# Two memory columns fewer, one guess fewer, and memory V turned by a transposing DMA, in a fused S5 scan and memory transformer kernel

## The chip, the cores and the metric

The kernel runs on one core of a Trainium2 chip. The metric is the device time of one execution in microseconds (us). A time is the median of an execution's repeats with the lowest and highest beside it. The span of a profile is some 1.7 us shorter than the time of the same execution.

Engine names: PE is TensorE (matmuls), PEld its weight loads, DVE VectorE, ACT ScalarE, POOL GpSimd, SP SyncE, which issues most DMAs here. "SPq" in a profile line is SP's sequencer.

## The reference, cut to what matters

```python
# A: S5 scan.  x is 2048 x 1024
h_t = Lam_bar * h_{t-1} + B_bar x_t ;  y = 2 Re(h C^T) + x * Dskip
# B: memory transformer.  64 segments of 32 rows, 8 memory rows, 32 heads x 128
mem = mem0
for s in range(64):
    h = concat([mem, x[32*s : 32*s+32]])            # 40 rows
    q, k, v = h @ Wq, h @ Wk, h @ Wv                # per head
    o = softmax(mask(q k^T / sqrt(128))) v  @ Wo
    mem = o[:8]; outs.append(o[8:])
return concat([y, concat(outs)], axis=-1)
```

Part B looks sequential. The kernel guesses each segment's memory with a linear formula from the segment means, computes all segments at once, checks the guess at the end, and only if the check fails branches into a slow general path. With these inputs the branch is never taken into that path.

## The kernel before

The memories are columns of a tile `memT` beside the 2048 columns of x. There are `NM` = 73 of them: 66 that belong to groups (22 groups of three segments) and 7 that are shared. Only 71 memories really exist; two columns are fillers. Three places multiply by these columns. The q and k projections have a tail of 201 = 128 + 73 columns. The memory V products have 73, and the guess products 64.

```python
NTL = 3 * NG; NMX = 7; NM = NTL + NMX               # 66, 7, 73
...
    def v_mem(self, hb, w=None):                     # memory V of a block of four heads
        k = self.k
        w = w or self.load_wv(hb)
        p = k.ps("P")
        for h in range(4):
            for c in range(KC):
                k.PE.matmul(p[:, h * NM:(h + 1) * NM], w[:, c, h * 128:(h + 1) * 128], self.memT[:, c, :], ...)
        vm = self.vmp.tile([128, 4, NM], BF16, name="b_vm", bufs=1)
        k.copy("v", vm[:], p[:, 0:4 * NM].rearrange("p (h n) -> p h n", h=4))
        yield
        pt = k.ps("P", (128, 1024), BF16)
        for h in range(4):                           # columns become rows: four PE transposes
            k.PE.transpose(pt[0:NM, h * 128:(h + 1) * 128], vm[:, h, :], k.ident[:])
        st = self.next_st()
        k.copy("v", st[0:NM, 0, :, 0:E], pt[0:NM, 0:512].rearrange("p (h e) -> p h e", h=4))
        sv = st[:, 0, :, :].rearrange("p h e -> p (h e)")
        k.SP.dma_start(self.vx[hb][64:64 + NMX, :], sv[0:NMX, :])
        k.SP.dma_start(self.vt[hb][:], sv[NMX:NM, :])
        yield
```

Attention then loads V of a head pair (two heads) from DRAM. For the first two head pairs the load begins with a zero fill of the 29 padding rows, by another DMA:

```python
    def load_v(self, hp):
            ...
            if hp < 2:                               # GW = 99: rows 99..127, 29 of them
                z = self.vx[0][T + 32:T + 32 + 128 - GW, 0:2 * EW].unsqueeze(1).to_broadcast([128 - GW, NG, 2 * EW])
                k.tc.keep_in_program_order(k.SP.dma_start(vt[GW:128, :, :], z))
            ...
            k.tc.keep_in_program_order(k.SP.dma_start(vt[0:GX, :, :], self.vx[hb]...))   # b_v <- b_vx
            k.SP.dma_start(vt[GX:GW, :, :], self.vt[hb]...)                              # b_v <- b_vt
```

The memory V of blocks 0 and 1 is computed before attention starts, that of blocks 2 to 7 inside it.

The scheduler moves independent instructions within an engine's stream, so the order on the chip is not the order of the source everywhere.

Of the kernel before, what the change touches and what calls it, by code (L numbers as in the profile page):

```python
# [33 lines left out]
NTL = 3 * NG  # L34
NMX = 7
NM = NTL + NMX
# [300 lines left out]
class PartB:  # L337
    def __init__(self, k, x, mem0, Wq, Wk, Wv, Wo, out):
        self.k = k
        self.x, self.mem0, self.out = x, mem0, out  # L340
        self.Wf = [w.rearrange("(c p) h e -> p c (h e)", p=128) for w in (Wq, Wk, Wv)]
        self.Wo = Wo.rearrange("h e d -> e h d")
        self.vx = [k.drp.tile([NSLOT, 4 * EW], BF16, name=f"b_vx{i}") for i in range(HB)]
        self.vt = [k.drp.tile([NTL, 4 * EW], BF16, name=f"b_vt{i}") for i in range(HB)]
        self.on = [k.drp.tile([T, 1024], BF16, name=f"b_on{i}") for i in range(4)]
        self.tn = [k.drp.tile([NR, 1024], BF16, name=f"b_tn{i}") for i in range(4)]
        c = k.cst
        self.m0T = c.tile([128, KC, M], BF16, name="b_m0T")
        self.gx = c.tile([128, KC, NM], BF16, name="b_gx")
        self.vmp = c  # L350
        self.xbar = c.tile([128, KC, NSEG], BF16, name="b_xbar")
        self.ogT = c.tile([128, H, NSEG], BF16, name="b_ogT")
        self.accE = c.tile([128, HP * NU], FP32, name="b_accE")
        self.accR = c.tile([128, HP * 2 * NG], FP32, name="b_accR")
        self.flag = c.tile([1, 1], I32, name="b_flag")
# [19 lines left out]
    def fill(self, tmp):  # L375
        k = self.k
        z = tmp.tile([32, 4 * EW], BF16, name="b_xr", bufs=4)
        k.V.memset(z[:], 0.0)
        for hb in range(HB):
            k.SP.dma_start(self.vx[hb][64 + NMX:GX, :], z[0:GX - 64 - NMX, :])  # L380
            k.SP.dma_start(self.vx[hb][T + 32:NSLOT, :], z[0:32, :])
        for q in range(4):
            k.SP.dma_start(self.tn[q][NM:NR, 0:4 * EW], z[0:NR - NM, :])
            k.SP.dma_start(self.tn[q][NM:NR, 1024 - 4 * EW:1024], z[0:NR - NM, :])
# [116 lines left out]
    def og(self, hb, w, tag="R"):  # L501
        k = self.k
        p = k.ps(tag)
        late = tag != "R"
        for h in range(4):
            for c in range(KC):
                mm = k.PE.matmul(p[:, h * NSEG:(h + 1) * NSEG], w[:, c, h * 128:(h + 1) * 128], self.xbar[:, c, :], start=(c == 0), stop=(c == KC - 1))
                if late and h == 0 and c == 0:
                    k.tc.keep_in_program_order(mm)
        k.copy("s" if late else "v", self.ogT[:, hb * 4:(hb + 1) * 4, :], p[:, 0:4 * NSEG].rearrange("p (h s) -> p h s", h=4))  # L510
# [7 lines left out]
    def guess(self, pool):  # L518
        k = self.k; V, PE = k.V, k.PE
        pg = k.ps("S")  # L520
        for q in range(4):
            wo = self.wog.pop(0)
            for dc in range(2):
                c = 2 * q + dc
                for h in range(H):
                    PE.matmul(pg[:, c * NSEG:(c + 1) * NSEG], wo[:, h, dc * 128:(dc + 1) * 128], self.ogT[:, h, :], start=(h == 0), stop=(h == H - 1))
# [4 lines left out]
        V.tensor_copy(m[:, :, NMX + 3:NM], pv[:, :, 1:NSEG])  # L531
# [3 lines left out]
        V.tensor_copy(gx[:, :, 2:NTL - 1], pv[:, :, 1:NSEG])  # L535
        V.tensor_copy(gx[:, :, NTL - 1:NM], pv[:, :, 0:1].to_broadcast([128, KC, NMX + 1]))
        yield


    def v_mem(self, hb, w=None):  # L540
# [6 lines left out]
        vm = self.vmp.tile([128, 4, NM], BF16, name="b_vm", bufs=1)  # L547
        k.copy("v", vm[:], p[:, 0:4 * NM].rearrange("p (h n) -> p h n", h=4))
        yield
        pt = k.ps("P", (128, 1024), BF16)  # L550
        for h in range(4):
            k.PE.transpose(pt[0:NM, h * 128:(h + 1) * 128], vm[:, h, :], k.ident[:])
# [4 lines left out]
        k.SP.dma_start(self.vt[hb][:], sv[NMX:NM, :])  # L557
# [7 lines left out]
    def qk_zero(self, i):  # L565
        V = self.k.V
        for t in self.qk[i]:
            V.memset(t[:, :, 64 + NMX:GX], 0.0)
            V.memset(t[:, :, 21 * GP + 64:21 * GP + GX], 0.0)
            V.memset(t[:, :, 0:NG * GP].rearrange("p h (g n) -> p h g n", n=GP)[:, :, :, GW:GP], 0.0)  # L570
            V.memset(t[:, :, NG * GP:QW], 0.0)
# [9 lines left out]
    def proj(self):  # L581

        k = self.k; PE = k.PE
        for hp in range(HP):
# [5 lines left out]
            for i in range(2):  # L590
                t = self.qk[hp % 2][i]
                p = k.ps("P")
                for hh in range(2):
                    for c in range(KC):
# [3 lines left out]
                k.copy("v", t[:, :, 0:64], pv[:, :, 0:64])  # L598
                k.copy("v", t[:, :, 21 * GP:21 * GP + 64], pv[:, :, 64:128])
                k.copy("v", t[:, :, 64:64 + NMX], pv[:, :, 128:128 + NMX])  # L600
                k.copy("v", t[:, :, 0:NG * GP].rearrange("p h (g n) -> p h g n", n=GP)[:, :, :, GX:GW],
                       pv[:, :, 128 + NMX:NS].rearrange("p h (g j) -> p h g j", j=3))
# [45 lines left out]
    def att_back(self, blocks):  # L648
# [24 lines left out]
        if b0 + n == 2 * NG:  # L673
# [8 lines left out]
            k.SP.dma_start(tn[NTL:NM, cs], ov[64:64 + NMX, 0, :])  # L682
# [112 lines left out]
    def check(self):  # L795
# [9 lines left out]
        sq = pool.tile([128, 2, KC, NM], FP32, name="c_sq", bufs=1)  # L805
        df = pool.tile([128, 4, NM], FP32, name="c_df", bufs=1)
        for half in range(2):
            cs = slice(4 * half, 4 * half + 4)
            p = k.ps("P")
            for c in range(4):  # L810
                for h in range(H):
                    PE.matmul(p[:, c * NM:(c + 1) * NM], self.wo[half][:, h, c * 128:(c + 1) * 128], self.omT[:, h, 0:NM],
                              start=(h == 0), stop=(h == H - 1))
            pv = p[:, 0:4 * NM].rearrange("p (c n) -> p c n", c=4)
# [4 lines left out]
        ss = pool.tile([128, 2, NM], FP32, name="c_ss", bufs=1)  # L819
# [5 lines left out]
        for i in range(2):  # L825
            PE.matmul(pd[0:NM, i:i + 1], ss[:, i, :], onef[:], start=True, stop=True)
        t2 = small("c_t2", 2)
        V.memset(t2[:], 0.0)
        V.tensor_copy(t2[0:NM, :], pd[0:NM, 0:2])
# [145 lines left out]
def kernel_main(tc, A_x, A_Lre, A_Lim, A_Bre, A_Bim, A_Cre, A_Cim, A_logdt, A_Dskip, B_x, B_mem0, B_Wq, B_Wk, B_Wv, B_Wo, out,  # L975
                force=False, dbg=None):
    with ExitStack() as ctx:
# [128 lines left out]
        for n, (hp, u) in enumerate(at):  # L1106
            if n == 12:
                k.SP.dma_start(wo0[:], b.Wo[:, :, 0:512])
            if hp % 2 == 0 and 2 < hp + 2 < HP:
                if u == 4:  # L1110
                    vm = b.v_mem(hp // 2 + 1)
                if u in (4, 6):
# [109 lines left out]
```

## Time and profile before

| | before |
|---|---|
| time, median of 3 (lowest to highest) | 1247.11 us (1246.69 to 1247.39) |
| span of the profile | 1245.3 us |
| PE busy | 1234.2 us (99%) |
| DVE, ACT, POOL busy | 54%, 21%, 22% |
| stage 1 of the scan starts on PE | 35.7 us |
| attention | about 440 to 1060 us |
| last matmul ends | 1239.28 us |

From the page of the kernel before: the busy line of its first part, then the two lines of the chain of work that ended last (by engine, then by line).

```profile
PE 1234.2 (99%) x8270; PEld 662.5 (53%) x8342; DVE 667.7 (54%) x1250; ACT 263.4 (21%) x631; POOL 275.8 (22%) x407
...
PE 99%; issue 0%; DVE 0%
PE psP L64 82%; PE psU L64 9%; PE psS L64 3%; PE psO L64 2%; PE psR L64 2%; DVE b_xe L91 0%; DVE b_ost L91 0%; DVE a_n L962 0%; DVE hpb L105 0%; DVE ones L102 0%
```

Both say the same: the kernel is a queue of matmuls. Only less PE work, or less idle time of PE, makes it shorter. The view of waits on PE has one entry of any size, early in the kernel (columns: us in total, times, longest).

```profile
PE psR L64 <- DVE hpb L105: 1.3, 1, 1.3
```

The timeline of PE around one block's transposes (columns: start, us, engine, line, operation, output<-input, shapes, count) gives what a transpose costs in the stream. A duration includes the pipeline's depth, so the cost is read from one start to the next: four transposes take 571.10 - 570.88 = 0.22 us, 55 ns each, not 219 ns.

```profile
570.71 0.33 PE L64 MATMUL psO<-b_v,b_m 128*128 128x129 bf16 x3
570.88 0.39 PE L64 MATMUL psP<-ident,b_vm 128*73 128x128 bf16 x4
571.10 0.60 PE L64 MATMUL psP<-b_xe,b_wk 128*128 128x201 bf16 x5
```

SP's timeline in the same place shows the slack for the DMAs that follow. The memory V of a block is stored at 571.92 and 572.27 us, SP issues nothing between 573.4 and 589.0 us, and V is loaded only at 592.31 us.

```profile
571.92 0.30 SPq L64 DMA_DIRECT2D b_vx<-b_vst  x1
572.27 0.32 SPq L64 DMA_DIRECT2D b_vt<-b_vst  x1
...
572.98 0.40 SPq L64 DMA_DIRECT2D b_wv<-in_B_Wv_dram  x1
589.03 2.01 SPq L64 DMA_DIRECT2D b_on<-b_ob  x2
...
592.31 0.45 SPq L64 DMA_DIRECT2D b_v<-b_vx  x1
```

Two more stretches turned out to matter, and the prediction did not look at them. The first is SP's timeline at the start of attention: the first V load and its zero fill (together `b_v<-b_vx x2`) hold SP for 16.42 us, directly after the stores of memory V.

```profile
465.02 0.27 SPq L64 DMA_DIRECT2D b_vx<-b_vst  x1
465.34 0.29 SPq L64 DMA_DIRECT2D b_vt<-b_vst  x1
465.73 0.26 SPq L64 DMA_DIRECT2D b_v<-b_vt  x1
466.03 16.42 SPq L64 DMA_DIRECT2D b_v<-b_vx  x2
```

```profile
SPq L1156 <- SPq L1156: 2.8, 1, 2.8
```

### The profile page before, as it was taken

The numbers are of one execution on the slowest core, as the hardware profiler recorded it, in microseconds if no ns is written. First come the engines' busy times: TensorE is split into PE (matmuls) and PEld (weight loads), VectorE is DVE, ScalarE is ACT, GpSimd is POOL, SyncE is SP. The second block draws the span as 40 slices with busy tenths as digits, with TensorE's granted clock in tenths as the row PEclk, the third lists the DMA queues.
The fourth block names the chain that finished last, engine by engine and source line by source line (L and its number), as shares of the span: only waits on it lengthen the run. The fifth ranks groups of instructions, "written<-read, shape, count | busy, mean of one in ns | idle before, by whom it ended". The sixth has DMA issues, their size and how long they took to land.

```text
span 1245.3 us, 20124 instructions
## 1 busy us (share of the span) xinstructions
PE 1234.2 (99%) x8270; PEld 662.5 (53%) x8342; DVE 667.7 (54%) x1250; ACT 263.4 (21%) x631; POOL 275.8 (22%) x407
## 2 busy tenths in 40 slices
PE   9999999999999999999999999999999999999998
PEld 5444444444455555556666656555665554446444
DVE  4688899998711124666666666666666641001000
ACT  5344444443310000211112111111211110000000
POOL 4111331212332321322222222222222220000000
PEclk9999999999999999999999999999999999999999
DMA  9965444554898734664454545545553379407000
GB/s 248 272 191 147 131 135 127 144 155 107 242 322 248 249 116 95 196 170 124 96 145 108 144 108 120 132 92 121 120 142 92 65 211 230 107 18 153 17 26 19
DMA packets 316246, 176.83 MB, mean 142 GB/s; under 512 B 138874, under 2 KB 301550, under 8 KB 316150
## 3 DMA queue, kind: packets, MB, share of 16 engines
q1 hardware_dynamic: 294054, 147.95, 47.8%
q10 hardware_dynamic: 21072, 24.38, 5.9%
q0 software_dynamic: 1024, 3.17, 0.7%
q8 instruction: 66, 1.08, 0.4%
q14 instruction: 30, 0.25, 0.1%
HBM read 89.14 MB, written 53.17 MB: 114 GB/s over the span
## 4 chain that ended last, share of the span: by engine, by line
PE 99%; issue 0%; DVE 0%
PE psP L64 82%; PE psU L64 9%; PE psS L64 3%; PE psO L64 2%; PE psR L64 2%; DVE b_xe L91 0%; DVE b_ost L91 0%; DVE a_n L962 0%; DVE hpb L105 0%; DVE ones L102 0%
## 5 line engine op out<-in xcount | busy, mean ns | idle before, releaser
L64 PE MATMUL psP<-b_xe,b_wq 128*128 128x480 bf16 (+1 forms) x1280 | 247.7, 343 | 0.1
L64 PE MATMUL psP<-b_xe,b_wk 128*128 128x480 bf16 (+1 forms) x1280 | 247.7, 343 | 0.0
L64 PE MATMUL psP<-b_wv,b_xe 128*128 128x512 bf16 (+2 forms) x1033 | 223.4, 372 | 0.8
L644 POOL TENSOR_TENSOR b_m<-b_e,maskB 99x396 bf16<-99x396 bf16 x160 | 139.8, 874 | 338.5 <-ACT b_e L641 338.5
L641 ACT ACTIVATE b_e<-psS 99x396 bf16<-99x396 f32 x176 | 88.2, 501 | 536.7 <-PE psS L64 533.4
L64 PEld LDWEIGHTS <-b_wk 128*128 128x128 bf16 x1280 | 119.4, 98 | 94.2
L64 PEld LDWEIGHTS <-b_wq 128*128 128x128 bf16 x1280 | 118.7, 98 | 87.7
L64 PEld LDWEIGHTS <-b_xe 128*128 128x128 bf16 x1056 | 101.8, 98 | 119.1 <-DVE b_xe L91 0.2
L91 DVE CAST b_k<-psP 128x480 bf16<-128x480 f32 (+1 forms) x192 | 97.4, 528 | 100.9 <-PE psP L64 100.9
L91 DVE CAST b_q<-psP 128x480 bf16<-128x480 f32 (+1 forms) x192 | 97.4, 528 | 93.1 <-PE psP L64 91.5
L64 PEld LDWEIGHTS <-b_ol 128*128 128x128 bf16 x864 | 84.3, 98 | 94.4
L64 PE MATMUL psU<-a_xT,a_bt 128*128 128x512 bf16 x493 | 113.9, 379 | 1.1
L64 PE MATMUL psP<-t,a_hl 128*128 128x512 bf16 x496 | 112.1, 379 | 0.8
L91 DVE CAST b_ost<-psP 128x512 bf16<-128x512 f32 (+1 forms) x17 | 11.5, 676 | 177.4 <-PE psP L64 176.3
L64 PE MATMUL psP<-wo,b_ol 128*128 128x512 bf16 (+1 forms) x440 | 91.9, 364 | 0.4
L64 PE MATMUL psP<-t,b_ol 128*128 128x512 bf16 x408 | 91.7, 379 | 0.4
L280 POOL TENSOR_SCALAR a_tt<-a_pr,a_tabf 128x1 f32<-128x1 f32 x48 | 34.1, 710 | 243.2 <-DVE a_pr L275 243.2
L661 DVE TENSOR_TENSOR b_ob<-psO,b_accR 99x384 bf16<-99x384 f32 x160 | 85.9, 553 | 2.4 <-DVE b_accR L660 0.4
L89 ACT ACTIVATE b_vst<-psP 128x512 bf16<-128x512 f32 x126 | 71.9, 589 | 71.3 <-PE psP L64 59.9
L267 DVE TENSOR_TENSOR a_pr<-psU,a_tabf 128x2048 f32<-128x2048 f32 x32 | 73.0, 2282 | 15.7 <-PE psU L64 14.0
L64 PEld LDWEIGHTS <-a_bt 128*128 128x128 bf16 x512 | 49.2, 98 | 57.6
L64 PEld LDWEIGHTS <-a_hl 128*128 128x128 bf16 x512 | 49.0, 98 | 56.7
(200 smaller groups left out, 962.7 us busy)
## 6 DMA issues: line engine op xcount, KB each, us to landing
b_v<-b_vx SPq DMA_DIRECT2D x16, 1122.0 KB
b_wv<-in_B_Wv_dram SPq DMA_DIRECT2D x16, 1024.0 KB
b_vx<-b_vst ACTq DMA_DIRECT2D x24, 544.0 KB
b_on<-b_ob SPq DMA_DIRECT2D x15, 720.0 KB
a_hs<-a_h SPq DMA_DIRECT2D x32, 256.0 KB
b_wog<-in_B_Wo_dram SPq DMA_DIRECT2D x4, 2048.0 KB
b_wq<-in_B_Wq_dram SPq DMA_DIRECT2D x16, 512.0 KB
b_wk<-in_B_Wk_dram SPq DMA_DIRECT2D x16, 512.0 KB
```

The source lines that it names most:

```text
L64: r = f(*a, **kw)
L89: self.S.activation(out, in_, ACT.Copy)
L91: self.V.tensor_copy(out, in_)
L267: V.tensor_tensor(pr[:], u[:].unsqueeze(1).to_broadcast([128, 2, 2, TB]), view(t3, [[TB + 1, 2], [TB + 1, 2], [1, TB]]), ALU.mult)
L280: G.tensor_scalar(tt[:, j:j + 1], w[:, j, TB - 1:TB], t3[:, 1, TB:TB + 1], None, ALU.mult)
L641: k.S.activation(e[:], s[0:GW, :, :, 0:GW], ACT.Exp, scale=float(E) ** -0.5, accum_out=self.accE[0:GW, i:i + 1])
L644: k.G.tensor_tensor(m[0:GW, 0:4 * GP].rearrange("p (a b q) -> p a b q", a=2, b=2)[:, :, :, 0:GW], e[:], mask[0:GW, :, :].unsqueeze(2).to_b ...
L661: V.tensor_tensor(self.ob[:, b0:b0 + n, :], o[0:GW, 0:n, 0:E], r.unsqueeze(2).to_broadcast([GW, n, E]), ALU.mult)
```

## The change

The intent is to take work from PE. (1) The two filler columns go: 71 memory columns instead of 73. (2) The last segment's guess isn't needed: 63 guess columns instead of 64. (3) For six of the eight head blocks the four PE transposes are replaced by a store of V to DRAM, a transposing DMA back, and the stores. Because the filler columns are gone, memory V is no longer one contiguous run of rows, so its store becomes three (`store_t`).

```diff
-NM = NTL + NMX
+NT4 = NMX + 4
+NM = NMX + NSEG                     # 71
+NO = NTL + NMX                      # 73, for the check
 ...
+        self.vmt = [k.drp.tile([E, 512], BF16, name=f"b_vmt{i}") for i in range(HB)]
 ... fill(): eight small stores of ones for the filler rows of vt
-    mm = k.PE.matmul(p[:, h * NSEG:(h + 1) * NSEG], ..., self.xbar[:, c, :], ...)
+    mm = k.PE.matmul(p[:, h * NSEG:h * NSEG + NSEG - 1], ..., self.xbar[:, c, 0:NSEG - 1], ...)
 ... guess(): likewise 63 columns, and the copies out of PSUM cut to fit
+    def store_t(self, hb, s):
+        for r0, n, i in ((0, 2, NMX), (NTL - 3, 2, NMX + 2), (3, NTL - 6, NT4)):
+            self.k.SP.dma_start(self.vt[hb][r0:r0 + n, :].rearrange("n (h e) -> n h e", h=4), s[i:i + n, :, :])
 ... v_mem():
-        vm = self.vmp.tile([128, 4, NM], BF16, name="b_vm", bufs=1)
-        k.copy("v", vm[:], p[:, 0:4 * NM]...)
+        vm = self.vmp.tile([128, 4, 128], BF16, name="b_vm", bufs=1)
+        k.copy("v", vm[:, :, 0:NM], p[:, 0:4 * NM]...)
+        if hb > 1:
+            k.V.memset(vm[:, :, NM:128], 0.0)
+            k.SP.dma_start(self.vmt[hb][:], vm[:].rearrange("p h n -> p (h n)"))
+            yield
+            s = self.next_st()...
+            k.V.memset(s[:, :, E:EW], 1.0)
+            k.SP.dma_start_transpose(s[:, :, 0:E], self.vmt[hb][:])
+            yield
+            k.SP.dma_start(self.vx[hb][64:64 + NMX, :]..., s[0:NMX, :, 0:EW])
+            self.store_t(hb, s[:, :, 0:EW])
+            yield
         yield
         ... (blocks 0 and 1: PE transposes as before)
-        k.SP.dma_start(self.vt[hb][:], sv[NMX:NM, :])
+        self.store_t(hb, st[:, 0, :, :])
 ... proj(): the copies of the q and k tails re-cut, still four each
-                if u in (4, 6):
+                if u in (4, 6, 8):
                     next(vm)
```

More of the change, by code (lines that the diff above doesn't have):

```diff
@@ L348, in __init__ @@
         self.m0T = c.tile([128, KC, M], BF16, name="b_m0T")
-        self.gx = c.tile([128, KC, NM], BF16, name="b_gx")
+        self.gx = c.tile([128, KC, NO], BF16, name="b_gx")
         self.vmp = c
@@ L378, in fill @@
         k.V.memset(z[:], 0.0)
+        one = tmp.tile([2, 4 * EW], BF16, name="b_one", bufs=1)
+        k.V.memset(one[:], 1.0)
         for hb in range(HB):
@@ L381, in fill @@
             k.SP.dma_start(self.vx[hb][T + 32:NSLOT, :], z[0:32, :])
+            k.SP.dma_start(self.vt[hb].rearrange("(g j) n -> g j n", j=3)[0:NG:NG - 1, 2, :], one[:])
         for q in range(4):
-            k.SP.dma_start(self.tn[q][NM:NR, 0:4 * EW], z[0:NR - NM, :])
-            k.SP.dma_start(self.tn[q][NM:NR, 1024 - 4 * EW:1024], z[0:NR - NM, :])
+            k.SP.dma_start(self.tn[q][NO:NR, 0:4 * EW], z[0:NR - NO, :])
+            k.SP.dma_start(self.tn[q][NO:NR, 1024 - 4 * EW:1024], z[0:NR - NO, :])
     def load_x(self, q):
@@ L506, in og @@
             for c in range(KC):
-                mm = k.PE.matmul(p[:, h * NSEG:(h + 1) * NSEG], w[:, c, h * 128:(h + 1) * 128], self.xbar[:, c, :], start=(c == 0), stop=(c == KC - 1))
+                mm = k.PE.matmul(p[:, h * NSEG:h * NSEG + NSEG - 1], w[:, c, h * 128:(h + 1) * 128], self.xbar[:, c, 0:NSEG - 1], start=(c == 0), stop=(c == KC - 1))
                 if late and h == 0 and c == 0:
                     k.tc.keep_in_program_order(mm)
-        k.copy("s" if late else "v", self.ogT[:, hb * 4:(hb + 1) * 4, :], p[:, 0:4 * NSEG].rearrange("p (h s) -> p h s", h=4))
+        k.copy("s" if late else "v", self.ogT[:, hb * 4:(hb + 1) * 4, 0:NSEG - 1],
+               p[:, 0:4 * NSEG].rearrange("p (h s) -> p h s", h=4)[:, :, 0:NSEG - 1])
     def load_wog(self, q, pool):
@@ L520, in guess @@
         pg = k.ps("S")
+        NS = NSEG - 1
         for q in range(4):
@@ L525, in guess @@
                 for h in range(H):
-                    PE.matmul(pg[:, c * NSEG:(c + 1) * NSEG], wo[:, h, dc * 128:(dc + 1) * 128], self.ogT[:, h, :], start=(h == 0), stop=(h == H - 1))
+                    PE.matmul(pg[:, c * NSEG:c * NSEG + NS], wo[:, h, dc * 128:(dc + 1) * 128], self.ogT[:, h, 0:NS], start=(h == 0), stop=(h == H - 1))
                 yield
@@ L530, in guess @@
         V.tensor_copy(m[:, :, NMX + 1:NMX + 2], pv[:, :, 0:1])
-        V.tensor_copy(m[:, :, NMX + 3:NM], pv[:, :, 1:NSEG])
+        V.tensor_copy(m[:, :, NMX + 2:NT4], pv[:, :, NS - 2:NS])
+        V.tensor_copy(m[:, :, NT4:NM], pv[:, :, 1:NS - 2])
         gx = self.gx
         V.tensor_copy(gx[:, :, 0:2], pv[:, :, 0:2])
-        V.tensor_copy(gx[:, :, 2:NTL - 1], pv[:, :, 1:NSEG])
-        V.tensor_copy(gx[:, :, NTL - 1:NM], pv[:, :, 0:1].to_broadcast([128, KC, NMX + 1]))
+        V.tensor_copy(gx[:, :, 2:NTL - 2], pv[:, :, 1:NS])
+        V.tensor_copy(gx[:, :, NTL - 2:NO], pv[:, :, 0:1].to_broadcast([128, KC, NMX + 2]))
         yield
+    def store_t(self, hb, s):
+        for r0, n, i in ((0, 2, NMX), (NTL - 3, 2, NMX + 2), (3, NTL - 6, NT4)):
+            self.k.SP.dma_start(self.vt[hb][r0:r0 + n, :].rearrange("n (h e) -> n h e", h=4), s[i:i + n, :, :])
     def v_mem(self, hb, w=None):
@@ L546, in v_mem @@
                 k.PE.matmul(p[:, h * NM:(h + 1) * NM], w[:, c, h * 128:(h + 1) * 128], self.memT[:, c, :], start=(c == 0), stop=(c == KC - 1))
-        vm = self.vmp.tile([128, 4, NM], BF16, name="b_vm", bufs=1)
-        k.copy("v", vm[:], p[:, 0:4 * NM].rearrange("p (h n) -> p h n", h=4))
+        vm = self.vmp.tile([128, 4, 128], BF16, name="b_vm", bufs=1)
+        k.copy("v", vm[:, :, 0:NM], p[:, 0:4 * NM].rearrange("p (h n) -> p h n", h=4))
+        if hb > 1:
+            k.V.memset(vm[:, :, NM:128], 0.0)
+            k.SP.dma_start(self.vmt[hb][:], vm[:].rearrange("p h n -> p (h n)"))
+            yield
+            s = self.next_st()[:].rearrange("p i h e -> p (i h e)")[:, 0:576].rearrange("p (h e) -> p h e", h=4)
+            k.V.memset(s[:, :, E:EW], 1.0)
+            k.SP.dma_start_transpose(s[:, :, 0:E], self.vmt[hb][:])
+            yield
+            k.SP.dma_start(self.vx[hb][64:64 + NMX, :].rearrange("n (h e) -> n h e", h=4), s[0:NMX, :, 0:EW])
+            self.store_t(hb, s[:, :, 0:EW])
+            yield
         yield
@@ L551, in v_mem @@
         for h in range(4):
-            k.PE.transpose(pt[0:NM, h * 128:(h + 1) * 128], vm[:, h, :], k.ident[:])
+            k.PE.transpose(pt[0:NM, h * 128:(h + 1) * 128], vm[:, h, 0:NM], k.ident[:])
         st = self.next_st()
@@ L570, in qk_zero @@
             V.memset(t[:, :, 0:NG * GP].rearrange("p h (g n) -> p h g n", n=GP)[:, :, :, GW:GP], 0.0)
+            V.memset(t[:, :, GX + 2:GW], 0.0)
+            V.memset(t[:, :, 21 * GP + GX + 2:21 * GP + GW], 0.0)
             V.memset(t[:, :, NG * GP:QW], 0.0)
@@ L597, in proj @@
                 pv = p[:, 0:2 * NS].rearrange("p (h n) -> p h n", h=2)
-                k.copy("v", t[:, :, 0:64], pv[:, :, 0:64])
-                k.copy("v", t[:, :, 21 * GP:21 * GP + 64], pv[:, :, 64:128])
+                tg = t[:, :, 0:NG * GP].rearrange("p h (g n) -> p h g n", n=GP)
+                te = tg[:, :, 0:NG:NG - 1, :]
+                k.copy("v", te[:, :, :, 0:64], pv[:, :, 0:128].rearrange("p h (g n) -> p h g n", g=2))
                 k.copy("v", t[:, :, 64:64 + NMX], pv[:, :, 128:128 + NMX])
-                k.copy("v", t[:, :, 0:NG * GP].rearrange("p h (g n) -> p h g n", n=GP)[:, :, :, GX:GW],
-                       pv[:, :, 128 + NMX:NS].rearrange("p h (g j) -> p h g j", j=3))
+                k.copy("v", te[:, :, :, GX:GX + 2], pv[:, :, 128 + NMX:128 + NT4].rearrange("p h (g j) -> p h g j", g=2))
+                k.copy("v", tg[:, :, 1:NG - 1, GX:GW], pv[:, :, 128 + NT4:NS].rearrange("p h (g j) -> p h g j", j=3))
                 yield
@@ L681, in att_back @@
             k.SP.dma_start(tn[0:NTL, :].rearrange("(g j) n -> j g n", j=3)[:, :, cs], ov[GX:GW, :, :])
-            k.SP.dma_start(tn[NTL:NM, cs], ov[64:64 + NMX, 0, :])
+            k.SP.dma_start(tn[NTL:NO, cs], ov[64:64 + NMX, 0, :])
     def att_init(self):
@@ L804, in check @@
         yield
-        sq = pool.tile([128, 2, KC, NM], FP32, name="c_sq", bufs=1)
-        df = pool.tile([128, 4, NM], FP32, name="c_df", bufs=1)
+        sq = pool.tile([128, 2, KC, NO], FP32, name="c_sq", bufs=1)
+        df = pool.tile([128, 4, NO], FP32, name="c_df", bufs=1)
         for half in range(2):
@@ L811, in check @@
                 for h in range(H):
-                    PE.matmul(p[:, c * NM:(c + 1) * NM], self.wo[half][:, h, c * 128:(c + 1) * 128], self.omT[:, h, 0:NM],
+                    PE.matmul(p[:, c * NO:(c + 1) * NO], self.wo[half][:, h, c * 128:(c + 1) * 128], self.omT[:, h, 0:NO],
                               start=(h == 0), stop=(h == H - 1))
-            pv = p[:, 0:4 * NM].rearrange("p (c n) -> p c n", c=4)
+            pv = p[:, 0:4 * NO].rearrange("p (c n) -> p c n", c=4)
             V.tensor_tensor(df[:], pv, self.gx[:, cs, :], ALU.subtract)
@@ L818, in check @@
             yield
-        ss = pool.tile([128, 2, NM], FP32, name="c_ss", bufs=1)
+        ss = pool.tile([128, 2, NO], FP32, name="c_ss", bufs=1)
         V.tensor_reduce(ss[:], sq[:].rearrange("p a c n -> p a n c"), AX.X, ALU.add)
@@ L825, in check @@
         for i in range(2):
-            PE.matmul(pd[0:NM, i:i + 1], ss[:, i, :], onef[:], start=True, stop=True)
+            PE.matmul(pd[0:NO, i:i + 1], ss[:, i, :], onef[:], start=True, stop=True)
         t2 = small("c_t2", 2)
         V.memset(t2[:], 0.0)
-        V.tensor_copy(t2[0:NM, :], pd[0:NM, 0:2])
+        V.tensor_copy(t2[0:NO, :], pd[0:NO, 0:2])
         ok = small("c_ok", 3)
```

## The prediction

> **What bounds the kernel now.** TensorE. The page gives PE 1234.2 of 1245.3 us busy (99%), clock 0.999; the chain that ended last is 99% PE. In the busy table by stretch, attention (440 to 1060 us) has PE 619.5 of 620 us, DVE 355.7, ACT 106.0, POOL 162.2, DMA share 0.54. The wait list has no wait of PE above 1.3 us. So time is won only by taking TensorE work away, and what is added elsewhere is free inside its slack.
>
> **Removed on TensorE.** The built instruction order shows PE's sequence unchanged except for:
> - 24 transposes of memory V (four in each of six head blocks). Listed durations (219 ns) overlap; on the timeline four start at 570.88 and the next group at 571.10 us, so 55 ns each: 24 x 55 = 1.3 us.
> - Columns: 512 tail projections of q and k 201 -> 199, 256 memory V products 73 -> 71, 256 + 256 guess products 64 -> 63: 2048 columns. Starts on timeline and chain: 64 columns 29.1 ns, 73 columns 33.7, 201 columns 86.9, 512 columns 215.9: about 0.42 ns a column plus 2.5 to 3.3 ns. The Trainium skill, "TensorE: Matmul & The Clock Gate", section "Wait — 56ns, not 53.3ns?", gives N/2.4 GHz + 2.5 ns; this trace agrees. None is at a floor, so 2048 x 0.42 = 0.9 us (0.6 to 1.3 if widths are rounded to a small multiple).
>
> Sum: 2.2 us, all on the chain.
>
> **Added.** In each of six head blocks: a 128 KB store of V, a transposing DMA of it, four stores for two (rows of 272 bytes), two small memsets, against a 0.39 us PSUM copy removed. On SP the transposing DMA waits until the store has landed (the skill, "DMA: Bandwidth & Descriptors", section "Two DMAs through the same engine are not ordered", demands that; the built order shows the wait). A comparable transposing DMA, that of the check, holds SP 1.28 us. Memory V is stored at 571.9 us; SP is then idle from 573.4 to 589.0 us, and V is loaded at 592.3 us for a head pair used some 20 us later. I estimate the chain to be 8 to 15 us longer; that fits, and a delayed V load should not reach PE. DVE has 40% free.
>
> **Predicted time.** 1247.1 - 2.2 = 1244.9 us; eight times in ten between 1243.6 and 1246.3. Chances: faster by over 2% 0.01, within 2% 0.97, slower by over 2% 0.02.
>
> **What would show the steps right.** PE busy about 2.2 us lower and its idle unchanged near 11 us; eight transposes of memory V left; the periods of 199, 71 and 63 columns lower by 0.8, 0.8 and 0.4 ns; head pairs with a removed turn shorter by some 0.28 us, the others by 0.03 us; V loads later by a few us at most, with no wait of PE on them.
>
> **What would make it wrong.** SP held by the wait for the transposing DMA until output stores, weight or V loads come late and PE waits (PE idle grows inside 560 to 960 us); the transposing DMA or its 272-byte rows slowing other transfers likewise; odd widths (63) costing as much as even ones or more, which leaves 1.3 to 1.8 us.

## More of the kernel before

The kernel ends with the branch on the check's flag:

```python
        f0 = nc.values_load(b.flag[0:1, 0:1], min_val=0, max_val=1)
        with tc.If(f0 == 1, preferred_fallthrough_block=True, label="general"):
            ...                                      # the general path
```

PE uses the first V load at 492.16 us; the trace shows nearly no wait there (0.13 us), but nothing in the busy shares says how little is spare.

```profile
491.85 0.34 PE L64 MATMUL psS<-b_q,b_k 128*128 128x99 bf16 x4
492.16 0.50 PE L64 MATMUL psO<-b_v,b_m 128*128 128x129 bf16 x6
```

The second is the end. These are SP's instructions of the branch's source line (columns: count, shortest/median/longest in ns, first and last start), and SP's wait after it. The branch starts at 1240.1 us, and SP's next instruction only at 1243.0 us.

```profile
L1156 SPq EVENT_SEMAPHORE  x8: 17/17/17, 1243.0 to 1243.5; - x8
...
L1156 SPq COMPARE_BRANCH  x1: 58/58/58, 1240.1 to 1240.1; - x1
```

## The result, and the profile after

| | before | after |
|---|---|---|
| time, median of 4 (lowest to highest) | 1246.99 (1246.69 to 1247.39) | 1244.46 (1244.44 to 1244.53) |
| span of the profile | 1245.3 | 1242.7 |
| stage 1 starts on PE | 35.7 | 36.2 |
| last matmul ends | 1239.28 | 1238.58 |
| from there to the end | 5.97 | 4.10 |

The ratio is 0.998, with a 95% interval of 0.9962 to 0.9997: within 2%, as predicted. The time fell by 2.5 us; the prediction had 2.2. That closeness says little about the reasons. The places of the same products in the two traces were compared, and the span's difference of 2.6 us cut into stretches:

| stretch (bounded by the same PE products in both) | before | after | difference |
|---|---|---|---|
| start to first product of stage 1 | 35.7 | 36.2 | +0.5 |
| to the first group of memory V products | 415.3 | 415.3 | 0.0 |
| to the third group (holds the start of attention) | 113.28 | 114.03 | +0.75 |
| third to eighth group (five blocks of two head pairs) | 337.83 | 336.23 | -1.60 |
| eighth group to the end of the last matmul | 337.14 | 336.80 | -0.34 |
| last matmul to the end | 5.97 | 4.10 | -1.87 |

Only the fourth, the fifth and part of the third row are the intended gain. The chain and the busy line of the page after:

```profile
PE 1232.5 (99%) x8246; PEld 660.8 (53%) x8318; DVE 668.7 (54%) x1266; ACT 263.5 (21%) x631; POOL 276.2 (22%) x407
...
PE 97%; DMA 2%; issue 0%; SPq 0%; DVE 0%
PE psP L66 80%; PE psU L66 9%; PE psS L66 3%; PE psO L66 2%; DMA b_v<-b_vx 2%; PE psR L66 2%; DMA b_xr<-in_B_x_dram 0%; SPq L66 0%; DVE b_ost L93 0%; DVE b_vm L565 0%
```

There are 24 matmul records fewer, which are the transposes. PE's busy time fell by 1.7 us and not by 2.2, and its idle time, span less busy time, fell from 11.1 to 10.2 us. A DMA, `b_v<-b_vx`, has entered the chain that ended last. The waits of PE name it too:

```profile
PE psR L66 <- DVE hpb L107: 1.3, 1, 1.3
PE psO L66 <- DMA b_v<-b_vx: 0.9, 1, 0.9
```

Its place is the start of attention. These are PE's timeline, with the idle time before a group and its releaser in brackets, and then SP's:

```profile
492.23 0.34 PE L66 MATMUL psS<-b_q,b_k 128*128 128x99 bf16 x4
493.45 0.50 PE L66 MATMUL psO<-b_v,b_m 128*128 128x129 bf16 x6 [0.88 <-DMA b_v<-b_vx]
```

```profile
465.42 0.26 SPq L66 DMA_DIRECT2D b_vx<-b_vst  x1
465.74 0.91 SPq L66 DMA_DIRECT2D b_vt<-b_vst  x3
466.75 0.25 SPq L66 DMA_DIRECT2D b_v<-b_vt  x1
467.04 16.35 SPq L66 DMA_DIRECT2D b_v<-b_vx  x2
```

The one store `b_vt<-b_vst` of 0.29 us has become three of 0.91 us. The V load begins 1.01 us later than before (467.04 against 466.03): some 0.6 us from the stores, the rest from the later start of the whole kernel, which PE shares.

Where the transposing DMA works, things went as predicted. SP's timeline after, in the block shown before:

```profile
568.39 0.54 SPq L66 DMA_DIRECT2D b_vmt<-b_vm  x1
...
570.50 1.74 SPq L66 DMA_TRANSPOSE b_vst<-b_vmt  x1
...
575.91 0.96 SPq L66 DMA_DIRECT2D b_vx<-b_vst  x1
576.92 2.29 SPq L66 DMA_DIRECT2D b_vt<-b_vst  x3
589.98 2.08 SPq L66 DMA_DIRECT2D b_on<-b_ob  x2
...
593.28 0.42 SPq L66 DMA_DIRECT2D b_v<-b_vx  x1
```

The chain store, transposing DMA, stores ends, as SP issues it, at 579.2 us instead of 572.6, with 14 us to spare before V is loaded. The transposing DMA is issued only after the store has landed; the Trainium skill, "DMA: Bandwidth & Descriptors", section "Two DMAs through the same engine are not ordered", asks for exactly that wait on the first DMA's semaphore. The trace agrees: the store's semaphore got the last of its sixteen counts at 570.33 us, and SP began the transposing DMA at 570.50. The stores that follow wait in the same way for the transposing DMA, `b_vst<-b_vmt`: 12.8 us in four waits of SP, and PE's list of waits has no entry that comes of them.

Last, the end. The branch and SP's wait after it, in the kernel after:

```profile
L1185 SPq EVENT_SEMAPHORE  x8: 17/17/17, 1240.0 to 1241.0; - x8
...
L1185 SPq COMPARE_BRANCH  x1: 58/58/58, 1239.4 to 1239.4; - x1
```

```profile
SPq L1185 <- SPq L1185: 1.0, 2, 0.5
```

The gap behind the branch is 0.5 us instead of 2.8. Of these 2.3 us some 0.5 come back as a second wait on the same line (the entry above counts two), so the stretch after the last matmul is 1.9 us shorter. The code of the end is the same in both kernels.

### The profile page after: what moved, and what is told of

It is laid out like the page before. It is cut to its first block, busy times and chain, and to the rows that moved or that the text cites. A ratio compares the mean times of both kernels' runs of the same rounds, so it can differ in the third digit from the quotient of the medians. Undisturbed runs are those within 1.5% of the kernel's fastest.

```text
span 1242.7 us, 20147 instructions
## 1 busy us (share of the span) xinstructions
PE 1232.5 (99%) x8246; PEld 660.8 (53%) x8318; DVE 668.7 (54%) x1266; ACT 263.5 (21%) x631; POOL 276.2 (22%) x407
## 4 chain that ended last, share of the span: by engine, by line
PE 97%; DMA 2%; issue 0%; SPq 0%; DVE 0%
PE psP L66 80%; PE psU L66 9%; PE psS L66 3%; PE psO L66 2%; DMA b_v<-b_vx 2%; PE psR L66 2%; DMA b_xr<-in_B_x_dram 0%; SPq L66 0%; DVE b_ost L93 0%; DVE b_vm L565 0%
```

## The experiments

The theory after reading the two traces: -2.1 us of PE work, +0.9 us for a V load made late by two extra stores, and -1.9 us at the end, which has nothing to do with the intent. The end would depend on where the branch stands in SP's instruction stream: place 589 before, 632 after, counted in the built program. The rivals: the wait comes from the transposing DMA or from the columns' other effects; the end is shorter because of what the change does to the data and the work; or the PE saving is something else than counted.

All kernels gave correct results. All of them were timed beside the kernel before on the same chip; its time is given in brackets with each group.

### First group: one part each, and the end (before: 1247.30, 1246.94 to 1248.15, 7 runs)

**b_pads**: the kernel before with 42 tiny stores on SP, spread over 14 head pairs, which moves the branch to place 635.

```diff
+        self.scr = k.drp.tile([48, 128], BF16, name="b_scr")
 ...
+            for j in range(3 * (hp < 14)):
+                k.SP.dma_start(self.scr[3 * hp + j:3 * hp + j + 1, :], ov[0:1, 0, 0:128])
```

> The kernel before, with 42 tiny stores (one row of 256 bytes each, three per head pair) added to the SP queue in its idle times, so that SP's instruction stream is about as long as in the changed kernel (the branch at the end stands at place 635 instead of 589; 632 in the changed kernel). Theory (the changed kernel's end is 1.9 us shorter only because SP's branch over the fallback code stands elsewhere in its stream and its target need not be fetched): the gap on SP between the branch and the next instruction falls from 2.9 us to about 0.5 us, and the kernel gets about 1.9 us faster (near 1245.1 us), with TensorE unchanged. Rival (the end is shorter because the changed DMA traffic lets the last store land sooner): the gap stays at 2.9 us and the time at 1247.0 us or a little above.

It took 1245.37 us (1244.92 to 1245.67), 0.9984 of the kernel before (0.9968 to 1.0001: the interval just reaches 1, but the ranges of the times are 1.3 us apart). Adding work made it 1.9 us faster. The third to eighth group is unchanged at 337.83 us; the gap after the branch is 0.48 us. SP's instructions of the branch's line:

```profile
L1159 SPq EVENT_SEMAPHORE  x8: 17/17/17, 1241.2 to 1242.3; - x8
...
L1159 SPq COMPARE_BRANCH  x1: 58/58/58, 1240.6 to 1240.6; - x1
```

So the end's gain is to be had without any part of the change.

**b_hint**: the kernel before with a branch hint on SP as well as on PE, some 27 us before SP's branch.

```diff
                         hint(k)
+                        hint(k, mybir.EngineType.SP)
```

> The kernel before, with a prefetch hint for SP's branch over the fallback code, put where TensorE already has one, some 20 us before the end. Theory (SP waits 2.9 us for the instructions behind its branch): the gap after SP's branch falls to about 0.5 us and the time by about 1.9 us, to about 1245.1 us. Rival (the last store's landing or other traffic sets the end): nothing changes, 1247.0 us.

It took 1247.28 us (1247.12 to 1247.89), ratio 1.0002, and the gap stayed at 2.69 us. The hint ran at 1212.8 us and the branch at 1240.3 us. The hope of mending the stall with a hint missed. Why it doesn't work at that place is open: the trace has no packet of instructions on queue 14, the only queue of instructions besides PE's (see b_pad128), between the hint and 1241.28 us, so no fetch is seen to follow it. The hint moves the branch to place 590, still a slow one.

**a_cols**: the changed kernel with PE transposes in all blocks, so the columns alone.

```diff
-        if hb > 1:
+        if hb > 99:
 ...
-                    next(vm)
+                    next(vm, None)
```

> The changed kernel with memory V of all head blocks turned on TensorE as before; only the columns stay. Theory: the stretch between the first memory V products of two neighbouring even head pairs, 67.56 us before and 67.25 us in the changed kernel, is about 67.48 us (column saving 0.08 us of the 0.31 us, transposes 0.22 us), so TensorE in attention is about 1.3 us longer than in the changed kernel; the wait of 0.9 us of TensorE for the first V load stays, because the two extra stores per head block before that load stay; the period of 63 columns stays that of 64 (29.1 ns). Rival (the transposing DMA delays the first V load): the wait of 0.9 us is gone.

It took 1246.28 us (1245.64 to 1248.19), ratio 0.9996. Five blocks take 337.35 us, 0.48 less than before: 0.096 us a block. PE's waits, in this kernel without a single transposing DMA of memory V in it:

```profile
PE psO L66 <- DMA b_v<-b_vx: 0.9, 1, 0.9
```

The wait stays. So the transposing DMA isn't its cause. In the changed kernel the first store of `b_vmt` is issued only at 568.4 us, long after this wait.

**b_turn**: the kernel before with the transposing DMA alone, 73 columns and a single store of `vt`.

```diff
+        if hb > 1:
+            k.V.memset(vm[:, :, NM:128], 0.0)
+            k.SP.dma_start(self.vmt[hb][:], vm[:].rearrange("p h n -> p (h n)"))
+            ...  as in the change, but one store of vt:
+            k.SP.dma_start(self.vt[hb][:].rearrange("n (h e) -> n h e", h=4), s[NMX:NM, :, 0:EW])
```

> The kernel before with the transposing DMA for the last six head blocks as the only change (73 columns, one store of the tail rows). Theory: 67.56 us becomes about 67.34 us (24 transposes of 55 ns: 1.3 us in all); no wait of TensorE for the first V load beyond the 0.1 us of before; DMA and SP stay in their slack. Rival (the transposing DMA brings the 0.9 us wait): the wait is there.

It took 1244.87 us (1244.68 to 1245.95), ratio 0.9984 (0.9967 to 1.0000). Its list of PE's waits, which leaves out what is shorter than 0.15 us, has no `b_v<-b_vx`. The timeline still shows a short one:

```profile
492.88 0.34 PE L64 MATMUL psS<-b_q,b_k 128*128 128x99 bf16 x4
493.36 0.50 PE L64 MATMUL psO<-b_v,b_m 128*128 128x129 bf16 x6
```

The two starts are 0.48 us apart, against 0.17 in a_vpad below, where nothing is waited for: a wait of 0.3 us. The kernel before, read in the same way, has 0.1, the changed kernel 1.05; b_pads, with no part of the change, has 0.4. So small waits come and go; one of about 1 us appears only in kernels with the two extra stores. Five blocks take 336.70 us, 1.13 less than before, so 0.226 us for four transposes, 56.5 ns each. The branch stands at place 612 and the gap is 0.48 us: much of the 2.4 us is the end again. The two parts together, 0.096 + 0.226 = 0.322 us a block, give 1.61 for five blocks; the changed kernel shows 1.60.

### Second group: the wait, and the branch's place (before: 1246.70, 1246.39 to 1247.14, 9 runs)

**b_store**: the kernel before with the store of `vt` split in three for blocks 0 and 1, nothing else.

```diff
-        k.SP.dma_start(self.vt[hb][:], sv[NMX:NM, :])
+        for r0, r1 in ((0, 2), (2, 4), (4, NTL)) if hb < 2 else ((0, NTL),):
+            k.SP.dma_start(self.vt[hb][r0:r1, :], sv[NMX + r0:NMX + r1, :])
```

> The kernel before with the store of the 66 tail rows of V split in three for head blocks 0 and 1 alone, as the changed kernel does, with nothing else changed. Theory (the two extra stores of each block delay the first V load): a wait of TensorE for the first V load of 0.6 to 0.9 us appears near 493 us. Rival (the columns or the new rows of ones cause it): no such wait, as in the kernel before (0.1 us). SP's branch stands at place 593 instead of 589: slow end as before (gap 2.8 us) if the edge lies above 593, fast if below.

It took 1248.95 us in the profiled run and 1246.98 in the other, ratio 1.0010 (0.9992 to 1.0028). PE's timeline where the V load is first used:

```profile
491.94 0.34 PE L64 MATMUL psS<-b_q,b_k 128*128 128x99 bf16 x4
494.27 0.60 PE L64 MATMUL psO<-b_v,b_m 128*128 128x129 bf16 x6 [1.99 <-DMA b_v<-b_vx]
```

The wait came with the two extra stores alone. It was larger than in the changed kernel, 1.99 us (SP was held 17.43 us by the zero fill and the load, about 1 us longer than elsewhere), and it cost more than its length. These are the busy times in three stretches (columns: stretch, its length, busy time of PE, PEld, DVE, ACT and POOL with counts, granted clock, DMA share, GB/s):

```profile
490.00:494.54 4.54, 2.55 (x20) 1.38 (x19) 1.32 (x2) 0.59 (x2) 1.39 (x2) 1.00 0.99 239
494.54:497.95 3.41, 3.41 (x14) 1.42 (x11) 1.27 (x4) 0.00 (x0) 0.00 (x0) 0.50 0.07 22
497.95:500.00 2.05, 2.05 (x17) 1.19 (x16) 1.30 (x3) 0.59 (x2) 0.88 (x1) 1.00 0.07 22
```

The granted clock was 0.50 for 3.41 us, just after the wait, and 1.00 on either side. Half of 3.41 us is 1.7 us; with the 2.0 us by which the wait exceeds that of the kernel before, this is the 3.7 us by which the third group of memory V products came later in all. In the changed kernel a wait of 0.88 us cost nothing beyond itself: its group came 0.75 us late in that stretch. Why the longer wait lowered the clock was not tested. The run of 1246.98 us left no profile, but its listed mean clock is 1.000 against 0.998 here, and it is 2.0 us faster, which suggests that its clock did not drop. The branch stands at place 593 with a gap of 0.47 us, so this kernel's time hides an end that is 1.9 us shorter.

**a_vpad**: the changed kernel with the 29 padding rows zeroed by GpSimd (rows 96 to 127, before the loads fill 96 to 98 again) instead of the zero-filling DMA. The last line of the edit only keeps the output weights' load at its place in SP's order.

```diff
-                z = self.vx[0][T + 32:T + 32 + 128 - GW, 0:2 * EW].unsqueeze(1).to_broadcast([128 - GW, NG, 2 * EW])
-                k.tc.keep_in_program_order(k.SP.dma_start(vt[GW:128, :, :], z))
+                k.G.memset(vt[GX:128, :, :], 0.0)
 ...
-                k.SP.dma_start(wo0[:], b.Wo[:, :, 0:512])
+                k.tc.keep_in_program_order(k.SP.dma_start(wo0[:], b.Wo[:, :, 0:512]))
```

> The changed kernel with the zero rows 99 to 127 of the two V tiles set by GpSimd (rows 96 to 127, then the loads over them) in place of a load of 29 zero rows that stands ahead of the first V load and holds SP for 16 us; the load of the output weights is kept in program order so that it does not slip ahead. Theory (the first V load has no slack, because the zero-row load stands before it in SP's queue, and the two extra stores per head block pushed it past the point where TensorE needs it): the wait of TensorE of 0.9 us near 493 us is gone and nothing else changes, so about 1243.6 us, 0.9 us under the changed kernel, as long as the branch at the end of SP (place 630) stays in a good place. Rival (the wait comes from something that the columns change in the load itself, such as where its rows lie): the wait stays.

It took 1243.94 us (1243.77 to 1244.04, 5 runs), ratio 0.9978 (0.9964 to 0.9991), the best of all kernels here. SP and then PE at the start of attention:

```profile
465.62 0.91 SPq L66 DMA_DIRECT2D b_vt<-b_vst  x3
466.57 0.39 SPq L66 DMA_DIRECT2D b_v<-b_vx  x1
467.07 1.71 SPq L66 DMA_DIRECT2D b_v<-b_vt  x1
```

```profile
492.43 0.34 PE L66 MATMUL psS<-b_q,b_k 128*128 128x99 bf16 x4
492.60 0.50 PE L66 MATMUL psO<-b_v,b_m 128*128 128x129 bf16 x6
```

The three stores are still there, the wait is gone, and the last matmul ends at 1237.73 us instead of 1238.58, 0.85 us earlier (0.73 of it between the first and the third group, 0.12 from an earlier start). The two parts of the V load have also changed places in SP's order, which no run separates from the missing fill. The load of V holds SP for 0.39 us where the zero fill and the load had held it for 16.35. Why the fill is so slow is suggested by the DMA share of the changed kernel from 475 to 480 us, while SP is held:

```profile
475.00:480.00 5.00, 5.00 (x27) 2.42 (x25) 2.86 (x16) 0.00 (x0) 0.00 (x0) 1.00 0.09 27
```

A share of 0.09 of 16 DMA engines is 1.4 engines. That counts all queues; the view of the DMA queues in the same stretch has a share of 6.3%, or 1.0 engine, for the queue of SP's transfers (columns: packets, MB, share):

```profile
q1 hardware_dynamic: 172, 0.09, 6.3%
```

The Trainium skill, "DMA: Bandwidth & Descriptors", section "Why a DMA increments its semaphore by 16 and not by 1", says that such a DMA is spread over the largest number up to 16 that divides its outer sizes; 29 rows leave a single engine. The share of that queue agrees, and taking the fill away raised the share of all queues from 0.09 to 1.17 in the same stretch of this experiment, as other transfers could then move. (A share slightly above 1 can appear in this view.)

**b_pad8** and **b_pad128**: the kernel before with 8 and with 123 tiny SP stores, the edit of b_pads with other counts, to find how the end depends on the place. 8 stores give place 601; 123 give 717, which is 589 + 128.

```diff
+            for j in range([0, 0, 1, 1, 1, 1, 1, 1, 1, 1, 0, 0, 0, 0, 0, 0][hp]):      # b_pad8
+            for j in range([8, 8, 8, 8, 8, 8, 8, 8, 8, 8, 8, 8, 8, 8, 11, 0][hp]):      # b_pad128
+                k.SP.dma_start(self.scr[self.ns:self.ns + 1, :], ov[0:1, 0, 0:128])
+                self.ns += 1
```

> The kernel before with 8 tiny stores added on SP, branch at place 601. Places 589 and 590 gave a gap of 2.7 to 2.8 us after the branch, places 612 and up 0.5 us. Theory (an instruction block boundary between 590 and 612 decides): gap either 2.8 or 0.5 us, nothing between; tells where the edge lies.

> The kernel before with 123 tiny stores added on SP, so that the branch stands at place 717, exactly 128 after the slow place 589. Theory (instructions come in blocks of 128, the instruction queue moves 8192 bytes at a time): the gap after the branch is again 2.8 us. Rival (only the number of instructions or the traffic before the end matters, or blocks are larger): 0.5 us.

One run each: 1244.53 us with 8 stores, 1247.60 with 123. The gap after the branch is 0.47 us at place 601 and, at place 717, SP's instructions read:

```profile
L1161 SPq EVENT_SEMAPHORE  x8: 17/17/17, 1243.6 to 1244.2; - x8
...
L1161 SPq COMPARE_BRANCH  x1: 58/58/58, 1240.7 to 1240.7; - x1
```

All kernels together, by the branch's place in SP's stream, from their traces (a_slow and b_width are described below; b_fast and a_again, the programs of b_pad8 and of the changed kernel once more, have 0.5 too):

```
place   589  589  590  | 593  601  612  619  630  632  635  | 717  717
gap us  2.8  2.6  2.7  | 0.5  0.5  0.5  0.5  0.5  0.5  0.5  | 2.9  2.6
kernel  before, b_width, b_hint | b_store, b_pad8, b_turn, a_cols, a_vpad, after, b_pads | b_pad128, a_slow
```

So the gap goes with the place of the branch, whatever else the kernel does. Why it does is not shown. Two slow places lie 128 instructions apart; that is no proof of a period, as nothing beyond 717 and nothing between 635 and 717 was tried. The Trainium skill, "Runtime: NRT & Kernel Launch", section "Instruction fetch mechanics", says that a taken branch whose target isn't among the fetched pages forces a fetch before execution can go on. The jump over the general path, from place 589 to 708 in the kernel before, could be of that kind.

The DMA records neither prove nor refute it. They have packets of 16384 bytes on queue 8, and packets of 8192 bytes on queue 14. The 66 of queue 8, at 256 instructions each, are about PE's number of records (16,659 with its weight loads). The 30 of queue 14 within the span are far more than SP's 614 instructions need, so SP shares this queue with other engines and its own packets can't be told. Two packets of queue 14 come 1.0 to 1.3 us after SP's branch in the slow kernel before and in the fast changed kernel alike: in the fast one SP has long gone on, in the slow one it goes on 1.3 us after they have ended. The slow kernels have one more, but at 1243.58 us in the kernel before, 0.6 us after the gap is over, so SP did not wait for that one. The page's blocks are of 16 KiB, or 256 instructions, which fits the packets of queue 8; those of queue 14 are half as large.

### Third group: like against like, and the widths (before: 1246.78, 1246.43 to 1246.94, 7 runs)

**a_slow**: the changed kernel with 81 tiny SP stores, its branch at place 717, a slow one. **b_fast**: b_pad8 again, timed in rounds. **a_again**: the changed kernel itself, unedited. The edit of a_slow is that of b_pads with these counts:

```diff
+            for j in range(([0] + [5] * 14 + [11, 0])[hp]):
```

> The changed kernel with 81 tiny stores added on SP in its idle times, which puts SP's last branch at place 717 (it stands at 632), the place where the kernel before with 123 such stores was slow. Theory (1.9 us of the gain are the place of that branch, not the change): gap after the branch 2.8 us, time about 1.9 us above the changed kernel, so only 0.4 to 0.8 us under the kernel before. Rival (the gain belongs to the change): as the changed kernel, 1244.5 us.

> The kernel before with 8 tiny stores on SP (branch at place 601), again and timed, beside the changed kernel on the same chip. Theory: about 1.9 us under the kernel before (near 1244.9 us), so within 0.8 us of the changed kernel, which keeps only what TensorE saves less the wait for the first V load. Rival: no faster than the kernel before by more than 0.5 us.

> The changed kernel once more, on the same chip as the two runs before it and with another start. Theory: 2.0 to 2.6 us under the kernel before, wait of 0.5 to 1.2 us for the first V load, the same stretches in attention (336.2 us from the third to the eighth group of memory V products), gap of 0.5 us after SP's branch.

| branch at | without the change | with the change |
|---|---|---|
| a slow place | before: 1246.78 | a_slow: 1246.50 (1246.22 to 1246.63), ratio 0.9998 |
| a fast place | b_fast: 1244.49 (1244.41 to 1244.64), ratio 0.9982 | a_again: 1244.87 (1244.40 to 1245.06), ratio 0.9984 |

In rows of this table the branch's place is of the same kind, though not the same number (589 and 717; 601 and 632). The change is worth -0.3 us in the slow row and +0.4 us in the fast one; both intervals against the kernel before are wider than that, and the ranges overlap in both rows, so it is about nothing. The tiny stores are not quite free of side effects: b_pad128, at place 717 too, took 0.9 us more than the kernel before of its group in its single run, 0.6 us of them before the first group of memory V products, where PE once waits 0.5 us for a PSUM copy by ACT. In columns, the place is worth 2.3 and 1.6 us. Eight useless stores did what the whole change did. The stretches of the two profiles in the fast row, cut as in the table of the result, show how +0.6 us of span (1242.7 to 1243.3) comes about: start +0.9, to the first group of memory V products +0.4 (PE once waits 0.3 us there for a PSUM copy by ACT), to the third group +0.9, from the third to the eighth -1.6, to the last matmul -0.3, after it +0.3. The PE work is saved as before, -1.6 and -0.3, and given back elsewhere. a_again showed the wait (0.93 us), the stretch of 336.23 us and the gap of 0.47 us that were expected of it; its gain of 1.9 us is just under the 2.0 to 2.6 expected.

**b_width**: the kernel before with 64 extra products of each of twelve widths, back to back in one stretch.

```diff
+                if i == 25:
+                    pd = k.ps("S")
+                    for n in (64, 63, 62, 61, 74, 73, 72, 71, 202, 201, 200, 199):
+                        for j in range(64):
+                            mm = k.PE.matmul(pd[:, 0:n], wv[0][:, j % 8, ...], b.xe[:, j % 8, 0:n], start=True, stop=True)
+                            tc.keep_in_program_order(mm)
```

> The kernel before with 12 groups of 64 products added on TensorE before attention (results not used), of 64, 63, 62, 61, 74, 73, 72, 71, 202, 201, 200 and 199 columns. Theory (TensorE takes columns in pairs): 63 costs as 64, 61 as 62, 73 as 74, 71 as 72, 201 as 202, 199 as 200, with steps of 0.8 to 0.9 ns from pair to pair. Rival A (every column costs 0.42 ns): steps of 0.42 ns at each width. Rival B (columns in fours): 61 to 64 all alike, 201 costs 1.7 ns more than 200.

The time, 1284.64 us, is that of the added work. What counts are the distances of the starts, taken from the records (ns):

```
columns  64     63     62     61   |  74     73     72     71   |  202    201    200    199
ns       29.16  29.16  28.33  28.33|  33.79  33.89  32.44  32.51|  86.71  86.67  85.83  85.84
```

An odd width costs what the next even one costs. So 64 -> 63 saves nothing, 73 -> 71 saves 1.38 ns and 201 -> 199 saves 0.83 ns. The Trainium skill, "TensorE: Matmul & The Clock Gate", section "Wait — 56ns, not 53.3ns?", has N / 2.4 GHz plus about 2.5 ns: 29.17 ns for 64 columns and 86.67 for 202, which these records meet, but 28.75 for 63, which they do not. The measurement decides.

With these numbers the columns' saving is 512 x 0.83 + 256 x 1.38 + 512 x 0 = 0.78 us, and per block of two head pairs 64 x 0.83 + 32 x 1.38 = 97 ns; a_cols had 96 ns a block. With 24 x 56.5 ns = 1.36 us for the transposes, the PE work removed is 2.13 us.

### What stayed open: the start

Stage 1 begins on PE at 35.5 to 36.0 us in the eight kernels without the scratch `b_vmt` (the kernel before and seven experiments), and at 36.1 to 37.0 us in the six with it: after 36.2, a_again 36.4, a_cols 37.0, a_vpad 36.1, a_slow 36.6, b_turn 36.8. The first loads are issued at the same times, but the core's DMAs move 243 to 258 GB/s in the first 12 us of the six and 270 to 278 in the eight. PE waits up to 1.3 us for x and up to 0.6 us for Wv in most of the six (without the scratch, 0.5 and 0.2 in b_hint, and 0.8 and 0.3 for x in b_width and b_pad128). What the six share is the DRAM scratch and the wider tile `b_vm`, which could shift addresses; no run isolates it. As the ranges nearly touch, its size in one kernel is uncertain too: the same changed kernel had 36.2 and 36.4.

## Why the prediction was right or wrong

The time lay in the range, and the class was right. That the gain came within 0.3 us of the prediction was luck: of the four parts that make up the measured difference, the prediction had one, the work removed from PE.

- **PE bounds the kernel, and the work removed is 2.2 us on the chain: right in its total.** Measured 2.13. Transposes 56.5 ns (predicted 55). A block of two head pairs fell by 0.32 us (predicted 0.28 + 0.03 = 0.31).
- **The term of the columns was mis-sized.** Predicted 0.9 us at 0.42 ns for each of 2048 columns; measured 0.78. The step "63 instead of 64 columns" saves nothing, because widths go in pairs. The text had named that as a risk, with 1.3 to 1.8 us for what is left in that case; that was too low, as 73 -> 71 saves more than two columns' worth: 1.38 ns instead of 0.84.
- **The transposing DMA and its chain stay in the slack of SP: right.** The chain became 6.6 us longer, less than the 8 to 15 estimated, with 14 us to spare, and the stretch from the third to the eighth group, where all but one of these DMAs lie, is shorter by what PE no longer does.
- **"A delayed V load should not reach PE", "no wait of PE on them": wrong.** PE waits 0.9 us longer for the first V load. The prediction read the slack in the steady state (571 to 592 us) and took it for all V loads. At the start of attention there was none, and the change puts two stores directly ahead of that load (b_store has the wait, a_cols has it without the transposing DMA, b_turn has 0.3 us in all). Moving the slow zero fill away (a_vpad) takes the wait away although the stores stay.
- **"Its idle unchanged near 11 us": wrong.** It fell by 0.9 us, the sum of several changes. The end lost 1.9 us of a stall after SP's branch, and it did so because the change added 43 instructions to SP's stream. The prediction knew these as free because they lay in slack; what they moved was the place of the last branch. b_pads, b_pad8 and b_fast show it without any part of the change, and a_slow brings the stall back with the whole change in place.
- **The start became 0.5 us longer**, which the prediction didn't have; its cause is open.

In sum: -2.1 + 0.9 - 1.9 + 0.5 = -2.6 us in the span. Two things that were not predicted (+1.4) and one that was not either (-1.9) nearly cancelled. With the branch at a place of the same kind the change is worth between -0.3 and +0.4 us, within the scatter of the runs, so what the prediction costed correctly was given back at the start of attention and at the kernel's start.

The version that beats both is a_vpad: 1243.94 us, 2.8 us below the kernel before in its group. It owes 1.9 us or so of that to the branch's place; b_pad8, the kernel before at a fast place in the same group, had 1244.53 us in its single run, so 0.6 us are left for the change and the fill together.

## What to carry to other kernels

Before a gain of one or two parts in a thousand is believed, compare the kernels with their branches at places that are equally fast: add a few useless instructions to each engine's stream and see whether the time jumps; here eight tiny stores were worth 2.3 us, as much as a careful change. Slack has to be read at every place where a resource is used, above all at a stage's first use, where a queue that has no spare time looks like one that has. Price a narrower product by measuring the width itself, and look for DMAs over a number of rows that few engines can share, as the 29 here, ahead of a load that matters.

## What the Trainium skill lacked or had wrong

- "TensorE: Matmul & The Clock Gate", section "Wait — 56ns, not 53.3ns?": the formula has a cost for each column. The runs show pairs: 64 and 63 columns both 29.16 ns, 62 and 61 both 28.33, 202 and 201 86.7, 200 and 199 85.8. The steps aren't all alike either: 74 and 73 columns take 33.8 to 33.9 ns and 72 and 71 take 32.4 to 32.5, a step of 1.4 ns instead of 0.83.
- The same page, section "What's actually happening": the clock is said to fall to half after at least one idle window of about 3.4 us. In b_store it was 0.50 for 3.41 us, which is such a window's length, but after a wait of only 1.99 us; a wait of 0.88 us in the changed kernel was followed by no lower clock. After the last matmul of the fourteen profiles it fell 2.1 to 5.0 us later.
- "Runtime: NRT & Kernel Launch", section "Instruction fetch mechanics": it names the stall after a taken branch but no cost. If the gap seen here is that stall, which is not shown, it cost 2.8 us at a slow place against 0.5 us at a fast one. The page's blocks of 16 KiB are seen on queue 8 alone, PE's by the count above; the packets of queue 14 had 8192 bytes.
- No page says whether a branch hint on SP helps: b_hint, with the hint 27 us ahead of the branch, left the gap at 2.7 us.
- "DMA: Bandwidth & Descriptors", section "Why a DMA increments its semaphore by 16 and not by 1": the rule for the number of engines agrees with the share of 6.3%, or 1.0 engine, seen on the queue of SP's transfers here, but the section gives no time for how long such a DMA holds the queue that issues it. A fill of 29 rows and the load behind it held SP for 16.35 us; without the fill the load held it for 0.39 us.
